# A gated linear recurrence and a gated unit on one core: loads of 1024 tokens, exponentials in pairs, squares per chunk, and new instruction queues

## The chip, the cores and the metric

The kernel runs on one core of a Trainium2 chip. The core has a matrix engine (TensorE, PE in the profile; its weight loads are listed apart as PEld), three engines for elementwise work (VectorE or DVE, ScalarE or ACT, GpSimd or POOL), an engine that issues transfers (SyncE, SP) and 16 DMA engines. Each engine works through its own queue in order, and the queues meet at semaphores. The metric is the device time of one execution in microseconds (us), as the median of several runs. A profile comes from one execution, and its span is the time from the first to the last instruction.

## The reference

Inputs are x, r_gate and i_gate, each 4 sequences of 6336 tokens by 256 channels in float32, a parameter per channel, and the weights of a gated unit. What is computed:

```python
log_a = 8.0 * sigmoid(r_gate) * log(clip(sigmoid(a_param), 1e-6, 1 - 1e-6))
a_t = exp(log_a)
norm = sqrt(max(1 - a_t * a_t, 1e-6))
x_gated = norm * sigmoid(i_gate) * x
h = a_t[:, t] * h + x_gated[:, t]            # for every token t: y[:, t] = h
gate = sigmoid(sum over k of conv_w[k] * y shifted by 4 - k tokens)   # k = 0..4, causal
out = (gate * (y @ w_val)) @ w_out
```

The output is 4 x 6336 x 256 in float32. The inputs come to 78 MB and the output to 26 MB.

## The kernel before

All 25,344 tokens are one line, cut into 51 windows (256, 256, 512, then 512 each, the last 256 long) and 28 chunks. Chunks 0, 1 and 2 are one window, chunks 3 to 25 are two windows of 512, chunks 26 and 27 are one. Window w of chunk c is 2c - 3 or 2c - 2 in the middle. A gate or x is loaded by window with its tokens spread over the 128 partitions: a partition holds J = n/128 neighbouring tokens of 256 channels, 4 KB in one piece for a window of 512. The recurrence runs along tokens with channels on partitions, so a and the gated x are transposed on TensorE.

The whole order is written out in the string ORDER, one word for each step. A word is emitted onto the queue (or queues) of the engines it uses, so the words of an engine, read in the order of ORDER, are that engine's queue. The words, with their functions and lines:

- lr, li, lx (L292, SP): loads of the r gate, the i gate and x into rings of four windows each. st (L546, SP): the store of a window. All four share SP's one queue.
- ta, tb (L310, L313, ScalarE): tanh of the r gate and of the i gate of a chunk, into taring and tbring.
- tr (L357, TensorE): transposes of taring for a group of one or two chunks and one half h of the channels. ex (L378, ScalarE): the exponential of that group, out of PSUM into aring. It scales by khf, which s_kt computes from a_param at the start: a transpose on TensorE, a chain of small steps on VectorE and one exponential on ScalarE.
- sq (L386, GpSimd), sa (L394, ScalarE): squares of a, by chunk and half, into ering. rt (L405, ScalarE): square roots for a batch of up to three chunks. A switch between the table of tanh and exp and that of the square root is a table load (L562).
- pp (L320, GpSimd): adds 1 to the tanh of the i gate. up (L332, GpSimd): multiplies it by x into uring. xp (L337, TensorE) and uv (L346, VectorE) do the same for windows 1, 2 and 6 through PSUM.
- nt (L420, TensorE): transposes of the norms back to tokens. xg (L450, VectorE): multiplies uring by them. xt (L461, TensorE): transposes of the result. sc (L483, VectorE): the recurrence as a scan, by half.
- cv (L495, TensorE), tg (L502, ScalarE): convolution and its tanh. vl (L510, TensorE), gv (L515, VectorE): value matmuls and the gate's product. ou (L525, TensorE): output matmuls. cd (L533, VectorE) and ca (L535, ScalarE): copies of the result out of PSUM.
- wm (L364, TensorE): five matmuls that nobody reads, to keep TensorE warm. s_diag and s_wl, s_wcast prepare the weights of the convolution and of the matmuls.

An element of a transposed norm group is read as one column in nq, where nq is the number of 256-token pieces of a window:

```python
nc.tensor.transpose(out=bank[:, k:k + P], in_=ering[:, e + q:e + wins[w] // 2:nq], identity=ident[:])
```

With windows of 512, nq is 2, and the float32 columns that are read lie 8 bytes apart.

Of the kernel before, what the change touches and what calls it, by code (L numbers as in the profile page):

```python
# [40 lines left out]
ex.2.1 sq.1.0 ta.3 sq.2.1 pp.0 sq.0.0 sq.0.1 ta.4 tb.1 lr.10 tr.3.0@4,5 tb.2 lr.9 lr.8 lr.7 lx.2 tr.3.1@2,3 ex.3.0  # L41
s_wl.1 up.0 lx.1 lx.4 wm.10@6 ex.3.1 sq.3.0 wm.5@6 lx.3 wm.3@6 tb.3 sq.3.1 wm.9@6 wm.6@6 ta.6 pp.4 sq.4.1 ta.5 lr.13
li.5 xp.2@2,3 li.6 sq.4.0 li.7 lr.14 tr.5.0@4,5 lx.6 uv.2 pp.3 rt.0 rt.2 nt.0@0 up.4 xg.0 rt.1 xt.0@0,1 xp.1@2 rt.3
sc.0.0 nt.1@3 up.3 lx.5 nt.2@0 uv.1 s_wl.0 xg.1 xg.2 xt.1@2,3 sc.0.1 lx.7 sc.1.0 nt.3@6,7 lr.12 sc.1.1 xg.3 ex.5.0
xt.2@0,1 sc.2.1 sc.2.0 tb.4 cv.0@2,3 tr.5.1@4,5 xt.3@6,7 lr.11 li.8 sq.5.0 ex.5.1 tg.0 sc.3.0 pp.5 sc.3.1 cv.2@0,1
# [53 lines left out]
cv.48@0,1 st.44 cv.47@6,7 rt.11 xt.27@3 ou.46.0@4,5 xg.26 xg.27 ou.45.0@2,3 tg.47 sc.26.1 sc.26.0 vl.47@6,7 ca.46.0  # L99
gv.47 ca.45.0 tg.48 vl.48@4,5 cv.49@2,3 ou.47.0@0,1 tg.49 vl.49@6,7 sc.27.1 gv.48 sc.27.0 gv.49 st.46 ca.47.0  # L100
ou.48.0@4,5 ca.48.0 st.45 cv.50@0,1 tg.50 st.47 ou.49.0@6,7 ca.49.0 st.48 st.49 vl.50@4,5 gv.50 ou.50.0@4 ca.50.0
st.50
"""


@with_exitstack
def kernel(
# [82 lines left out]
    with tc.manual_schedule():  # L190
# [103 lines left out]
        def op_lr(w):  # L294
            load(w, "r")
# [298 lines left out]
```

## Time and profile before

| what | before |
| --- | --- |
| median of 3 runs | 287.52 us (287.51 to 288.32) |
| span of the profiled execution | 286.4 us (the page gives no other time of it) |
| ScalarE busy | 273.6 us, 96% |
| TensorE busy | 251.8 us, 88% |
| VectorE busy | 246.8 us, 86% |
| GpSimd busy | 241.6 us, 84% |
| bytes moved | 104.76 MB, mean 366 GB/s |

Busy time is a sum over the whole span; what counts in a stretch is read from the rows of that stretch. A row of a stretch gives its start and end, its length, each engine's busy time and instruction count, the granted TensorE clock, the share of time in which the DMA engines were busy and the rate. A row of a timeline gives start, length, engine, line, operation, tiles and shape, a count where neighbours are merged, and in brackets the idle time before it with what ended that. A row of a group gives busy us, the mean ns of one, and idle time. A wait row gives the total in us, how often, and the longest.

### The profile page before, as it was taken

How to read it: one execution, taken by the hardware profiler on the slowest of the kernel's cores; microseconds unless marked ns; L12 is line 12 of the kernel's file. 1: busy time of each engine (PE TensorE's matmuls, PEld its weight loads, DVE VectorE, ACT ScalarE, POOL GpSimd, SP SyncE). 2: the span in 40 equal slices, each digit the busy share in tenths (PEclk: the TensorE clock that was granted, in tenths of full speed). 3: DMA queues.
4: the chain of work that ended last, by engine and by line, in shares of the span. 5: the costliest groups of instructions: out<-in, count | busy, mean ns of one | idle time of the engine just before them, and what ended most of it. 6: DMA issues, size and time to landing. Idle time of an engine off the chain costs nothing.

```text
span 286.4 us, 6382 instructions
## 1 busy us (share of the span) xinstructions
PE 251.8 (88%) x2552; PEld 171.1 (60%) x2576; DVE 246.8 (86%) x214; ACT 273.6 (96%) x198; POOL 241.6 (84%) x161
## 2 busy tenths in 40 slices
PE   1387778899999999988988999989989899999993
PEld 1253447456656767455756676656646774767562
DVE  4002898969999899999999999999999999999991
ACT  5999999999999999999999999999999999898984
POOL 1659589899999999999999999999996999874600
PEclk9999999999999999999999999999999999999999
DMA  7999999999999999999999999999999999994536
GB/s 243 384 373 407 409 403 408 388 366 376 410 408 366 418 367 392 414 410 334 405 364 413 411 332 356 420 416 419 415 401 333 359 416 406 364 356 170 192 150 256
DMA packets 29996, 104.76 MB, mean 366 GB/s; under 512 B 3335, under 2 KB 3854, under 8 KB 29966
## 3 DMA queue, kind: packets, MB, share of 16 engines
q1 hardware_dynamic: 29952, 104.35, 94.5%
q8 instruction: 20, 0.33, 0.5%
q14 instruction: 10, 0.08, 0.1%
q10 hardware_dynamic: 14, 0.01, 0.0%
HBM read 78.39 MB, written 25.95 MB: 364 GB/s over the span
## 4 chain that ended last, share of the span: by engine, by line
ACT 33%; PE 29%; DVE 14%; issue 12%; DMA 8%; SPq 1%; ACTq 0%; DVEq 0%
ACT ering L405 8%; PE banks L495 8%; DVE yring L483 7%; PE banks L525 7%; DMA rring<-in_r_gate_dram 6%; ACT tgring L502 6%; ACT taring L310 5%; ACT tbring L313 5%; ACT aring L378 5%; PE banks L510 5%; PE banks L461 3%; DVE tgring L515 3%; PE banks L420 3%; ACT L562 3%; DVE oring L533 2%
## 5 line engine op out<-in xcount | busy, mean ns | idle before, releaser
L386 POOL TENSOR_TENSOR ering<-aring 128x1024 f32<-128x1024 f32 (+2 forms) x54 | 91.5, 1714 | 16.7 <-ACT aring L378 16.4
L332 POOL TENSOR_TENSOR uring<-tbring,xring 128x1024 bf16<-128x1024 bf16 (+1 forms) x48 | 101.1, 2119 | 3.6 <-DMA xring<-in_x_dram 3.1
L483 DVE TENSOR_TENSOR_SCAN yring<-aring,yring,banks 128x1024 bf16<-128x1024 f32 (+5 forms) x50 | 101.7, 2064 | 2.1 <-PE banks L461 1.9
L495 PE MATMUL banks<-yring,diag 64*64 64x512 bf16 (+7 forms) x1080 | 62.1, 361 | 2.3 <-ACT aring L378 1.6
L515 DVE SCALAR_TENSOR_TENSOR tgring<-tgring,banks 128x1024 bf16<-128x1024 bf16 (+1 forms) x51 | 59.1, 1178 | 4.0 <-PE banks L510 3.4
L320 POOL TENSOR_SCALAR tbring<-tbring 128x1024 bf16<-128x1024 bf16 (+1 forms) x48 | 49.1, 1032 | 6.8 <-ACT tbring L313 6.7
L378 ACT ACTIVATE aring<-banks,khf 128x2048 f32<-128x2048 bf16 (+3 forms) x38 | 54.2, 1476 | 0.4 <-PE banks L357 0.3
L525 PE MATMUL banks<-wo,tgring 128*128 128x256 bf16 x396 | 51.0, 274 | 3.7 <-DVE tgring L515 3.2
L502 ACT ACTIVATE tgring<-banks 128x1024 bf16<-128x1024 f32 (+1 forms) x51 | 50.2, 1011 | 2.0 <-PE banks L495 1.9
L510 PE MATMUL banks<-yring,wv 128*128 128x512 bf16 (+4 forms) x192 | 48.1, 359 | 3.7 <-ACT tgring L502 1.9
L310 ACT ACTIVATE taring<-rring 128x2048 bf16<-128x2048 f32 (+2 forms) x28 | 47.9, 1718 | 1.4 <-DMA rring<-in_r_gate_dram 1.4
L525 PEld LDWEIGHTS <-tgring 128*128 128x128 bf16 x396 | 41.2, 114 | 13.1 <-DVE tgring L515 8.8
L313 ACT ACTIVATE tbring<-iring 128x2048 bf16<-128x2048 f32 (+2 forms) x28 | 48.2, 1726 | 0.0
L405 ACT ACTIVATE ering<-ering 128x4096 bf16<-128x4096 f32 (+5 forms) x16 | 44.8, 2840 | 0.1
L495 PEld LDWEIGHTS <-diag 64*64 64x64 bf16 x1080 | 29.0, 106 | 25.6 <-issue 9.9
L533 DVE COPY oring<-banks 128x1024 f32<-128x1024 f32 (+1 forms) x36 | 41.9, 1182 | 1.4 <-PE banks L525 0.7
L357 PE MATMUL banks<-ident_b,taring 128*128 128x128 bf16 x396 | 29.9, 230 | 9.4 <-ACT taring L310 6.7
L357 PEld LDWEIGHTS <-taring 128*128 128x128 bf16 x396 | 26.5, 103 | 14.2 <-ACT taring L310 7.4
L510 PEld LDWEIGHTS <-wv 128*128 128x128 bf16 x216 | 19.7, 98 | 24.5 <-issue 10.3
L450 DVE TENSOR_TENSOR uring<-banks,uring 128x2048 bf16<-128x2048 bf16 (+2 forms) x26 | 29.4, 1134 | 3.5 <-PE banks L420 3.2
L420 PE MATMUL banks<-ident,ering 128*128 128x128 f32 x192 | 28.3, 289 | 1.1 <-ACT ering L405 0.9
L461 PE MATMUL banks<-ident,uring 128*128 128x128 f32 x192 | 25.9, 276 | 3.5 <-DVE uring L450 2.8
(49 smaller groups left out, 154.0 us busy)
## 6 DMA issues: line engine op xcount, KB each, us to landing
rring<-in_r_gate_dram SPq DMA_DIRECT2D x48, 512.0 KB, 8.2
iring<-in_i_gate_dram SPq DMA_DIRECT2D x48, 512.0 KB, 8.7
xring<-in_x_dram SPq DMA_DIRECT2D x48, 512.0 KB, 8.2
out_dram<-oring SPq DMA_DIRECT2D x48, 512.0 KB, 6.5
rring<-in_r_gate_dram SPq DMA_DIRECT2D x3, 256.0 KB, 4.1
iring<-in_i_gate_dram SPq DMA_DIRECT2D x3, 256.0 KB, 6.5
xring<-in_x_dram SPq DMA_DIRECT2D x3, 256.0 KB, 8.5
out_dram<-oring SPq DMA_DIRECT2D x3, 256.0 KB, 5.2
```

Source lines behind the costliest of these rows:

```text
L310: nc.scalar.activation(**tangent(c, taring, NTR, rring, NRI))
L313: nc.scalar.activation(**tangent(c, tbring, NTI, iring, NII))
L332: nc.gpsimd.tensor_tensor(out=u, in0=t1, in1=xt, op=ALU.mult)
L378: nc.scalar.activation(out=dst, in_=src, func=ACT.Exp, scale=khf[:, h:h + 1], bias=khf[:, h:h + 1])
L386: nc.gpsimd.tensor_tensor(out=e, in0=a, in1=a, op=ALU.mult)
L405: nc.scalar.activation(out=ering[:].bitcast(BF16)[:, 4 * o:4 * o + 2 * n], in_=ering[:, 2 * o:2 * o + 2 * n], func=ACT.Sqrt, scale=-0.25, ...
L483: nc.vector.tensor_tensor_scan(out=yring[:, h, col:col + o1 - o0], data0=aring[:, h, a_at[c] + o0:a_at[c] + o1], data1=xT[:, o0:o1], initi ...
L495: nc.tensor.matmul(out=gp[oh * 64:oh * 64 + 64, h, a:b], lhsT=diag[half * 64:half * 64 + 64, h, k, :], rhs=yring[half * 64:half * 64 + 64, ...
L502: nc.scalar.activation(out=tgring[:, w % NTG, :, 0:wins[w]], in_=live.pop(("gp", w))[:, :, 0:wins[w]], func=ACT.Tanh, scale=0.5)
L510: nc.tensor.matmul(out=val[:, m, a:b], lhsT=wv[:, hk, m * P:(m + 1) * P], rhs=yring[:, hk, col:col + b - a], start=(hk == 0), stop=(hk == ...
L515: nc.vector.scalar_tensor_tensor(out=tgring[:, w % NTG, :, 0:wins[w]], in0=tgring[:, w % NTG, :, 0:wins[w]], scalar=1.0, in1=live.pop(("va ...
L525: nc.tensor.matmul(out=ops[:, j * D:(j + 1) * D], lhsT=gv[:, hk, j:wins[w]:J], rhs=wo[:, hk, :], start=(hk == 0), stop=(hk == H - 1))
```

## The change

- A load takes a whole chunk: 1024 tokens, 1 MB, in one transfer, with 8 neighbouring tokens (8 KB) on a partition. There are 28 loads each of r, i and x instead of 51. Stores stay by window. The x ring takes its slots as the other rings do, at (w + 1) % 4.
- Tokens of a chunk therefore lie in another order: J = 8 where it was 4. tr, ex, nt and xt step accordingly. In nt and xt, nq is that of a chunk, 4 where it was 2.
- Exponentials: chunks 11 and 12, and 21 and 22, were groups of one and are pairs. There are 34 exponentials instead of 38.
- Squares: from chunk 3 to 25 one instruction on GpSimd covers both halves of a chunk. The two squares on ScalarE, sa.25.1 and sa.27.1, go to GpSimd.
- pc adds 1 to the tanh for a whole chunk, and takes the place of 44 of the 48 pp.
- s_kt and s_diag take their PSUM bank from ORDER, and stand in other places.
- All of ORDER is new. Among its differences: 8 wm instead of 17, one copy (ca.35) on ScalarE instead of VectorE, r loads from lr.0 up.

```diff
-GROUPS = [[0], [1], [2], [3, 4], [5, 6], [7, 8], [9, 10], [11], [12], [13, 14], [15, 16], [17, 18], [19, 20], [21],
-    [22], [23, 24], [25], [26], [27]]
+GROUPS = [[0], [1], [2], [3, 4], [5, 6], [7, 8], [9, 10], [11, 12], [13, 14], [15, 16], [17, 18], [19, 20], [21, 22],
+    [23, 24], [25], [26], [27]]
 ORDER = """
-s_ident s_small s_kt s_diag lr.2 lr.0 s_wl.3 lr.1 li.0 lr.3 s_wl.2 ta.2 ta.0 lr.4 tr.0.1@0 tr.2.0@1 lr.6 ta.1 lr.5
-tr.1.0@2 tb.0 tr.0.0@3 li.1 tr.2.1@4 ex.2.0 li.2 tr.1.1@5 li.3 ex.1.1 lx.0 ex.0.1 sq.1.1 li.4 ex.1.0 sq.2.0 ex.0.0
+s_ident lr.0 lr.1 lr.2 s_small li.0 ta.0 lr.3 ta.1 tr.1.1@5 wm.4@7 tr.0.0@1 tr.0.1@0 tr.1.0@7 ta.2 s_kt@2 tb.0 ex.0.0
+tr.2.1@4 ex.2.1 ex.0.1 ex.1.0 lr.4 li.2 lx.0 wm.6@6 wm.1@7 tr.2.0@7 wm.2@4 sq.2.1 ta.3 ex.1.1 pp.0 sq.1.1 up.0 ta.4
+lr.5 lx.1 li.3 tr.3.0@0,1 s_wl.1 s_wl.3 lx.2 li.1 s_wl.0 s_wl.2 lx.3 ex.2.0 tb.2 ex.3.0 sq.2.0 sq.0.1 sq.1.0 sq.0.0
+tr.3.1@4,5 ex.3.1 ta.5 tb.3 tb.1 lr.6 li.4 s_diag@6 xp.2@0,1 xp.1@4 sq.4 sq.3 uv.2 rt.1 rt.0 rt.2 uv.1 nt.1@5 xg.1
...
+        def load(c, which):
+            w, k, n = cwins[c][0], len(cwins[c]), clen[c]
+            ring, slots = {"r": (rring, NRI), "i": (iring, NII), "x": (xring, NX)}[which]
+            at = place(w, slots)
+            dst = ring[:, at:at + k, 0:wins[w] // P, :].rearrange("p w j d -> p (w j) d")
+            nc.sync.dma_start(dst, flat[which][cstart[c]:cstart[c] + n, :].rearrange("(p j) d -> p j d", p=P))
...
+        def op_pc(c):
+            w, k = cwins[c][0], len(cwins[c])
+            t = tbring[:, place(w, NTI):place(w, NTI) + k, 0:wins[w] // P, :].rearrange("p w j d -> p (w j d)")
+            nc.gpsimd.tensor_scalar(out=t, in0=t, scalar1=1.0, scalar2=1.0, op0=ALU.mult, op1=ALU.add)
...
+        def both_squares(c):
+            n = clen[c]
+            return (ering[:, H * e_at[c]:H * (e_at[c] + n)].rearrange("p (h n) -> p h n", h=H),
+                    aring[:, :, a_at[c]:a_at[c] + n])
+
+        def op_sq(c, *h):
+            e, a = squares(c, h[0]) if h else both_squares(c)
             nc.gpsimd.tensor_tensor(out=e, in0=a, in1=a, op=ALU.mult)
...
         def op_nt(c, *at):
             bank = banks[:, at[0]:at[-1] + 1].rearrange("p b n -> p (b n)")
+            k, n = 0, clen[c]
+            nq = n // (2 * P)
+            for q in range(nq):
+                for h in range(H):
+                    e = live["n", c] + h * n // 2
+                    nc.tensor.transpose(out=bank[:, k:k + P], in_=ering[:, e + q:e + n // 2:nq], identity=ident[:])
+                    k += P
...
+            nq = clen[c] // (2 * P)
             for h in range(H):
                 bank = banks[:, at[h]]
+                for u, q in pairs(c):
+                    nc.tensor.transpose(
+                        out=bank[:, q:clen[c] // 2:nq],
+                        in_=u[:, h * P:(h + 1) * P, :].rearrange("p d two -> p (d two)").bitcast(FP32),
+                        identity=ident[:])
```

The stretches of the queues that the prediction speaks of, in the new order:

- TensorE starts with tr.1.1 wm.4 tr.0.0 tr.0.1 tr.1.0 s_kt tr.2.1 wm.6 wm.1 tr.2.0 wm.2 tr.3.0 tr.3.1. Before: s_kt s_diag tr.0.1 tr.2.0 tr.1.0 tr.0.0 tr.2.1 tr.1.1 tr.3.0 tr.3.1.
- ScalarE starts with ta.0 ta.1 ta.2 s_kt tb.0 ex.0.0 ex.2.1 ex.0.1 ex.1.0 ta.3 ex.1.1 ta.4 ex.2.0 tb.2 ex.3.0 ex.3.1 ta.5 tb.3 tb.1 rt.1 rt.0 rt.2 rt.3. Before: s_kt ta.2 ta.0 ta.1 tb.0 ex.2.0 ex.1.1 ex.0.1 ex.1.0 ex.0.0 ex.2.1 ta.3 ta.4 tb.1 tb.2 ex.3.0 ex.3.1 tb.3 ta.6 ta.5 rt.0 rt.2 rt.1 rt.3.
- SP starts with lr.0 lr.1 lr.2 li.0 lr.3 lr.4 li.2 lx.0 lr.5 lx.1 li.3 s_wl.1 s_wl.3 lx.2 li.1 s_wl.0 s_wl.2 lx.3 lr.6 li.4.
- From rt.10 on, TensorE has nt.23 vl.41 vl.40 xt.23 ou.41 ou.39 nt.24 ou.40 cv.42 tr.27.0 vl.42 tr.27.1 nt.25 xt.24 cv.43 ... ou.49 vl.50 ou.50. Before: nt.23 vl.41 vl.40 nt.24 xt.23 ou.39 cv.42 ou.41 ou.40 vl.42 tr.27.1 xt.24 tr.27.0 cv.43 vl.43 nt.25 ... ou.49 vl.50 ou.50.

More of the change, by code (lines that the diff above doesn't have):

```diff
@@ L41 @@
[L41 to L45, printed above, removed]
@@ L103 @@
+ca.50.0 st.50
 """
@@ L229, in s_ident, with s_kt @@
             nc.gpsimd.tensor_copy(out=ident_b[:], in_=ident[:])
-        def s_kt():
-            kps = banks[:, 0]
+        def s_kt(at):
+            kps = banks[:, at]
             nc.tensor.transpose(out=kps[:, 0:H], in_=ap2[0:H, :], identity=ident[0:H, 0:H])
```

213 lines of the change are left out of this document (86 added, 127 removed).

## The prediction

> **What bounds the kernel now.** I read the page first, the span and the busy times.
>
> ```profile
> span 286.4 us, 6382 instructions
> PE 251.8 (88%) x2552; PEld 171.1 (60%) x2576; DVE 246.8 (86%) x214; ACT 273.6 (96%) x198; POOL 241.6 (84%) x161
> ```
>
> The span is 286.4 us; the runs' median is 287.52, so 1.1 us lies around the span, and I add it at the end. ScalarE (ACT) is busiest. Next the stretches, one row each (us; busy time and count per engine, then granted clock, DMA share, GB/s).
>
> ```profile
> 0.00:10.00 10.00, 2.66 (x19) 2.08 (x19) 3.80 (x20) 6.40 (x11) 1.70 (x9) 1.00 0.81 278
> 10.00:20.00 10.00, 5.67 (x39) 4.16 (x40) 0.00 (x0) 9.62 (x9) 6.55 (x8) 1.00 1.02 388
> 20.00:60.00 40.00, 32.63 (x313) 21.31 (x314) 29.68 (x30) 39.63 (x27) 34.64 (x25) 1.00 1.02 402
> 60.00:100.00 40.00, 38.62 (x358) 25.67 (x361) 36.17 (x27) 39.90 (x27) 39.94 (x25) 1.00 1.01 389
> 100.00:244.00 144.00, 134.85 (x1453) 92.36 (x1463) 141.92 (x109) 143.73 (x92) 140.74 (x86) 1.00 1.00 389
> 244.00:280.00 36.00, 35.46 (x365) 24.22 (x369) 34.51 (x29) 31.95 (x35) 18.05 (x13) 1.00 0.67 245
> ```
>
> To be seen: from 20 to 244 ScalarE hardly rests (143.7 of 144 us in the long stretch). Before 60 it idles 3.60 + 0.38 + 0.37 = 4.35 us, nearly all of it in the first 10. VectorE rests 3.8 us in 60 to 100 and 2.1 in the 144 after that; GpSimd is nearly as full (3.1 of 144 idle) and the transfers' share is 1.00. No engine has room, so the middle can become shorter only by less work on ScalarE. From 244 to 280 it is TensorE that is full, 35.46 of 36. The hand-over is in the timelines of ScalarE and TensorE (start, us, what):
>
> ```profile
> 238.87 5.33 ACT L405 ACTIVATE ering<-ering 128x6144 bf16<-128x6144 f32 x1
> ...
> 243.04 1.07 PE L525 MATMUL banks<-wo,tgring 128*128 128x256 bf16 x8
> 244.25 1.23 PE L420 MATMUL banks<-ident,ering 128*128 128x128 f32 x8
> ...
> 248.39 1.04 PE L461 MATMUL banks<-ident,uring 128*128 128x128 f32 x8
> ...
> 282.17 0.61 PE L525 MATMUL banks<-wo,tgring 128*128 128x256 bf16 x4 [0.84 <-DVE tgring L515]
> ```
>
> Square roots rt.10 end at 244.20, and at 244.25 TensorE starts nt.23, the transposes that need them. From there to 282.78 it works nearly without a gap: 38.5 us. Behind nt.23 its queue has the same instructions before and after the change, in another order. So the end is the end of rt.10, plus 38.5 us of TensorE, plus the last copy and store, 3.6 us. And rt.10 ends when ScalarE has done what stands ahead of it. So the sum is ScalarE's work and waits up to rt.10, then TensorE's work behind it.
>
> **ScalarE's work up to rt.10.** I compared the two queues word by word. Same set of tanh, square roots and table loads (14 ahead of rt.10's own, in both), with four differences. Rows (one of the timeline, then groups by shape with busy us and mean ns):
>
> ```profile
> 194.21 4.49 ACT L378 ACTIVATE aring<-banks,khf 128x1024 f32<-128x1024 bf16 x4
> ...
> L378 ACT ACTIVATE aring<-banks,khf 128x2048 f32<-128x2048 bf16 x18 | 36.8, 2074 | 0.0
> L535 ACT COPY oring<-banks 128x1024 f32<-128x1024 f32 x14 | 13.9, 1016 | 2.1 <-PE banks L525 2.0
> L378 ACT ACTIVATE aring<-banks,khf 128x1024 f32<-128x1024 bf16 x10 | 11.4, 1219 | 0.0
> ...
> L394 ACT ACTIVATE ering<-aring 128x1024 f32<-128x1024 f32 x1 | 1.1, 1122 | 0.0
> ```
>
> Four single exponentials in a row took 4.49, not 4 x 1.219 = 4.88, so neighbours overlap by 0.13. The eight single ones (chunks 11, 12, 21, 22) thus cost 8 x 1.09 = 8.7 us, four paired ones 4 x (2.074 - 0.13) = 7.8: **-0.9**. Square sa.25.1 leaves ScalarE, 1.12 - 0.13: **-1.0**. Copy ca.35 comes to it, 1.02 - 0.13: **+0.9**. The other square, sa.27.1, stood behind rt.10 and is worth nothing. The pairs now read PSUM at half the former step. Single ones read at that step already, and (2074 - 1219)/1024 = 0.83 ns per element says that the step is free: 0.
>
> **The start.** Every exponential needs khf, which s_kt makes. Before, s_kt heads TensorE's queue. Now it stands behind tr.1.1, wm.4 and three more tr, so it waits for ta.1, and ta.1 for a load. Rows of before (the ScalarE, VectorE, TensorE and SP timelines):
>
> ```profile
> 0.74 0.52 ACTq L224 DMA_DIRECT2D ap<-in_a_param_dram  x1
> 4.54 1.58 ACT L310 ACTIVATE taring<-rring 128x1024 bf16<-128x1024 f32 x2 [0.49 <-DMA rring<-in_r_gate_dram]
> ...
> 3.46 0.16 DVE L234 COPY ksig<-banks 128x2 f32<-128x2 f32 x1 [3.46 <-PE banks L233]
> 6.64 0.17 DVE L248 TENSOR_SCALAR khf<-ktmp 128x2 f32<-128x2 f32 x1
> ...
> 3.19 0.23 PE L233 MATMUL banks<-ident,ap 2*128 2x2 f32 x1 [3.19 <-DMA ap<-in_a_param_dram]
> 6.94 1.65 PE L357 MATMUL banks<-ident_b,taring 128*128 128x128 bf16 x14 [0.37 <-DVE wcol L256]
> 17.90 6.31 PE L364 MATMUL banks<-ident_b 128*128 128x512 bf16 x25
> ...
> 0.72 0.86 SPq L292 DMA_DIRECT2D rring<-in_r_gate_dram  x2
> ...
> L310 ACT ACTIVATE taring<-rring 128x512 bf16<-128x512 f32 x3 | 1.9, 621 | 0.2 <-DMA rring<-in_r_gate_dram 0.2
> DMA to landing us min/median/max: 3.8/8.0/11.1
> ```
>
> Loads now start with lr.0 and lr.1, issued at 0.72 and 1.15. The 768 KB of before had landed at 4.54; I take 3.8 for the first 256 KB and 4.4 for the second. ta.0 runs to 4.4 and ta.1 to 5.0 (0.62 each). Then TensorE: two transposes 0.24 (1.65/14 each), wm.4 1.26 (five of 6.31/25), six transposes 0.71, s_kt's own 0.23: 7.45. VectorE's chain took 3.46 to 6.81, 3.35 us, so khf is ready at 10.8. ScalarE stands meanwhile: its exponential inside s_kt is queued ahead of tb.0, and all behind that waits for khf. Done by 10.8 are one table load 1.28, ta.0 and ta.1 1.24, ta.2 1.06, that exponential 0.2, tb.0 0.63: 4.4. So it has idled 6.4 us, against 4.35 in the whole start of before: **+2.1**. Bounds: the 1 KB parameter, issued at 0.74, was used at 3.19, so nothing lands within 2.45 us; then lr.1 lands at 3.6, khf comes at 10.0 and the loss is 1.3. If each load takes the 3.8 us that is the least for this ring, khf comes at 11.4 and the loss is 2.6.
>
> Further waits in the start: lr.3 now fills two slots, one of them still held by lr.0, so it waits for ta.0 (before, its first half went out at once). lr.4 waits for ta.2, lr.5 for ta.3, and SP is in order, so li.2 and lx.0 queue behind. I followed it at 400 GB/s (1 MB in 2.6 us), with 2 us from issue to the first byte (1 KB took 2.45): lr.5 is issued at 14.7 and lands at 19.3 for ta.5 at 22.7; li.3 lands at 22 for tb.3 at 24.5; li.1 at 24.7 for tb.1 at 26.3. All in time, with 1.6 us as the least room. Squares of chunks 4 and 3 now wait for both halves (ex.3.1 ends at 22.7) and take 3.6 us each, so rt.3 could start at 29.9; ScalarE arrives at 30.3. Cost 0, up to 1.8 if the cover is gone.
>
> **The middle.** GpSimd, by shape:
>
> ```profile
> L386 POOL TENSOR_TENSOR ering<-aring 128x1024 f32<-128x1024 f32 x45 | 84.4, 1896 | 6.1 <-ACT aring L378 5.8
> L386 POOL TENSOR_TENSOR ering<-aring 128x512 f32<-128x512 f32 x4 | 4.2, 1039 | 2.9 <-ACT aring L378 2.9
> L320 POOL TENSOR_SCALAR tbring<-tbring 128x1024 bf16<-128x1024 bf16 x46 | 47.8, 1050 | 6.8 <-ACT tbring L313 6.7
> L320 POOL TENSOR_SCALAR tbring<-tbring 128x512 bf16<-128x512 bf16 x2 | 1.2, 619 | 0.0
> ```
>
> Squares cost 1.67 ns per element and 0.18 us per instruction, additions 0.84 ns and 0.19. One instruction in place of two saves 0.18 and 0.19 per chunk, 8 us over 22 chunks, less some 2 us for the two squares that come from ScalarE. ScalarE has no wait there that this could end: 0. VectorE loses one copy and does uv.2 and uv.1 earlier, beside idle time: 0, since ScalarE sets rt.10. Nine of 17 warming groups go, 11 us of TensorE; it has gaps there, and the clock stood at 1.00 in the stretch after the last of them: 0. Loads are half as many issues of twice the size. ScalarE waited 1.4 us in all for the r ring, and the start's waits are counted above: 0, with a price in the rivals.
>
> **The norm's transposes.** nt now reads ering at a step of 16 bytes, not 8 (one column in nq, and nq goes from 2 to 4). Groups of eight: nt.23 took 1.23 us, xt.23, which reads adjacent elements, 1.04.
>
> ```profile
> L420 PEld LDWEIGHTS banks<-ident,ering x192: 140/209/223, 28.5 to 258.1; 128*128 128x128 f32 x192
> L420 PE MATMUL banks<-ident,ering x192: 272/283/389, 28.6 to 258.2; 128*128 128x128 f32 x192
> ...
> L461 PEld LDWEIGHTS banks<-ident,uring x192: 137/141/152, 29.6 to 262.3; 128*128 128x128 f32 x192
> L461 PE MATMUL banks<-ident,uring x192: 270/273/329, 29.6 to 262.4; 128*128 128x128 f32 x192
> ```
>
> Less the last one (0.283 and 0.273), that is a pace of 0.135 and 0.110 us. Weight loads take 209 ns at 8 bytes and 141 adjacent. Doubling the step cost 0.025; from 8 to 16 bytes, by bytes spanned, twice that, 0.05. In the middle TensorE's gaps and the lost warming groups cover it. Behind rt.10 nothing does: 24 transposes (nt.23 to nt.25), **+1.2**. Bounds: 0 if the step no longer matters, 24 x 0.138 = 3.3 if the pace takes the whole growth of the weight load (two more times 69 ns). A gain is excluded, since 8 bytes are dearer than 4. [...] xt writes PSUM at double the step too; its matmuls that write adjacent words (chunks 0 and 1, nq = 1) are among the shortest, 270, and the median is 273: 0.
>
> **Sum.** -0.9 - 1.0 + 0.9 + 2.1 + 1.2 = +2.3 on the span: 288.7, and with 1.1 around it 289.8 us.
>
> **Rivals.**
>
> A, the forecast: khf late, transposes dearer, 289.8. Its own range goes from 288.4, where B ends, to 289.8 + 0.5 + 2.1 = 292.4, with both upper bounds. Chance 0.52.
>
> B, no change: the loss at the start is at its lower end (1.3) and the wider step is free: 287.52 - 1.0 + 1.3 = 287.8. For it speaks that the loss rests on landing times not seen alone. Chance 0.18. I call it no change within 0.3% (0.86 us), about what a measurement of this kernel can tell.
>
> C, loads become the bound. A slot pair must be empty before 1 MB can be asked for, x had single slots until now. By my walk 11.0 MB have landed at 33.3 us, where the rows of before give 2.78 + 3.88 + 5.35 = 12.0; and with a share of 1.00 to 1.02 at 389 to 402 GB/s the 2.5 us are hard to make good. Against it: SP itself waits on compute (its waits by releaser, then its and ScalarE's timelines, then the page's issues).
>
> ```profile
> SPq L292 <- ACT taring L310: 24.5, 11, 4.6
> ...
> 195.21 2.72 SPq L292 DMA_DIRECT2D rring<-in_r_gate_dram  x3
> ...
> 213.09 1.90 ACT L310 ACTIVATE taring<-rring 128x2048 bf16<-128x2048 f32 x1
> ...
> rring<-in_r_gate_dram SPq DMA_DIRECT2D x48, 512.0 KB, 8.2
> ```
>
> The three issues at 195.21 hold lr.44 and lr.43: out by 197.9 and landed some 8.2 later, 206, they had 7 us before ta.23 read them at 213.1. C decides when a load comes more than 7 us later than now. Then 0.1 us on each of some 40 r and i loads makes +4: 293.8. Chance 0.18.
>
> D, faster: GpSimd paced the middle, at 39.94 of 40 in 60 to 100, and ScalarE's full rows only follow it. Then it runs as fast as VectorE lets it, which rested 2.1 us in 100 to 244, and the start's loss is absorbed: 287.5 - 2.1 = 285.4. It decides if ScalarE has idle time in the middle of the new profile while the end comes earlier. Against it: ScalarE waits for nothing there, and its durations are work. Chance 0.12. [...]
>
> **Numbers.** Time 289.8. Faster is D, 0.12; same is B, 0.18; slower is A and C, 0.70. The range leaves out D and the far end of C: 287.0 to 294.0.
>
> **What would show it.** ScalarE idle near 6 us in the first 11, its first exponential near 10.8; rt.10 ending near 245.3; no idle over 0.5 us per 40 between 20 and 240; nt's weight loads well over 209 ns and a group of eight near 1.6 us; TensorE 39.7 us behind rt.10; GpSimd some 6 us less busy. Wrong if khf comes before 9.6, if ScalarE waits for rring or iring in the middle, or if nt keeps its 1.23.

## The result, and the profile after

The changed kernel takes 300.44 us in the median, against 287.92 for the kernel before on the same chip: 1.043 times as long, 95% interval 1.038 to 1.048. Of its four executions one, at 306.74 us, fell in a slower state (with it the median is 301.15); medians and ratios, here and below, are of the other, fast ones. I forecast 289.8 (287.0 to 294.0). The sign was right, the size was not: +12.5 us where I had +2.3. The profiled execution took 300.44 us, with a span of 298.7. First the page's busy times, then two rows of stretches: the whole time up to rt.10's first instruction, after and before (start:end, length, then busy time and count of PE, PEld, DVE, ACT and POOL, granted clock, DMA share, GB/s).

```profile
span 298.7 us, 6120 instructions
...
PE 249.0 (83%) x2531; PEld 169.8 (57%) x2531; DVE 247.4 (83%) x213; ACT 272.7 (91%) x193; POOL 237.7 (80%) x118
```

```profile
0.00:250.36 250.36, 206.51 (x2097) 141.43 (x2101) 207.49 (x180) 233.43 (x156) 213.18 (x103) 0.96 0.95 369
```

```profile
0.00:238.87 238.87, 209.36 (x2123) 142.69 (x2146) 206.44 (x181) 234.15 (x161) 218.42 (x146) 1.00 1.00 386
```

To be seen: up to rt.10, which starts 11.5 us later, ScalarE worked 0.7 us less than before (233.43 against 234.15) and stood still for 16.9 us instead of 4.7. Nearly all of the loss is waiting ahead of rt.10. What comes behind is about as long as before. The timeline of TensorE after:

```profile
255.75 1.23 PE L409 MATMUL banks<-ident,ering 128*128 128x128 f32 x8 [0.47 <-ACT ering L396]
...
293.91 0.61 PE L512 MATMUL banks<-wo,tgring 128*128 128x256 bf16 x4 [0.84 <-DVE tgring L502]
```

From nt.23's start to the last output matmul's end it is 38.8 us (38.5 before; I had forecast 39.7), and a group of eight norm transposes still takes 1.23. Where ScalarE waits is shown by its wait view (operation and what released it: us in total, times, longest) and its timeline, both of the changed kernel:

```profile
ACT taring L298 <- DMA rring<-in_r_gate_dram: 5.2, 3, 2.2
ACT aring L372 <- POOL ering L385: 4.6, 3, 1.9
ACT tgring L489 <- PE banks L482: 4.0, 5, 1.6
...
ACT aring L372 <- DVE khf L239: 2.3, 1, 2.3
```

```profile
6.94 1.06 ACT L298 ACTIVATE taring<-rring 128x1024 bf16<-128x1024 f32 x1 [2.23 <-DMA rring<-in_r_gate_dram]
...
11.47 2.14 ACT L372 ACTIVATE aring<-banks,khf 128x256 f32<-128x256 bf16 x4 [2.35 <-DVE khf L239]
...
39.05 0.60 ACT L489 ACTIVATE tgring<-banks 128x512 bf16<-128x512 f32 x1 [1.62 <-PE banks L482]
...
54.11 4.00 ACT L372 ACTIVATE aring<-banks,khf 128x2048 f32<-128x2048 bf16 x2 [1.06 <-POOL ering L385]
...
83.82 1.91 ACT L298 ACTIVATE taring<-rring 128x2048 bf16<-128x2048 f32 x1 [1.55 <-DMA rring<-in_r_gate_dram]
...
117.74 4.01 ACT L372 ACTIVATE aring<-banks,khf 128x2048 f32<-128x2048 bf16 x2 [1.85 <-POOL ering L385]
...
124.63 1.02 ACT L489 ACTIVATE tgring<-banks 128x1024 bf16<-128x1024 f32 x1 [1.08 <-PE banks L482]
...
243.31 1.20 ACT L372 ACTIVATE aring<-banks,khf 128x1024 f32<-128x1024 bf16 x1 [1.66 <-POOL ering L385]
...
250.36 5.33 ACT L396 ACTIVATE ering<-ering 128x6144 bf16<-128x6144 f32 x1
```

Three sorts of wait are new. In the first 12 us: ta.2 for its load and the first exponential for khf. ScalarE is busy 4.84 us there, 8.40 before (the rows of after and before):

```profile
0.00:12.00 12.00, 4.69 (x23) 2.37 (x24) 2.77 (x17) 4.84 (x8) 0.97 (x7) 1.00 0.78 268
0.00:12.00 12.00, 2.66 (x19) 2.08 (x19) 3.80 (x20) 8.40 (x13) 3.69 (x11) 1.00 0.84 295
```

Then exponentials that wait for GpSimd: 1.06, 1.85 and 1.66 us. And a handful of waits for the r ring (83.82) and for the convolution's matmuls (39.05, 124.63). These three sorts come to 3.6 + 4.6 + 4.2 = 12.4 us, about the 12.2 by which ScalarE stood still longer ahead of rt.10. The stretches of the middle say the same; where I had said "no idle over 0.5 us per 40", ScalarE lacks 1.9 to 3.0 us in three of four:

```profile
20.00:60.00 40.00, 28.76 (x254) 19.11 (x254) 27.59 (x30) 37.26 (x26) 30.64 (x18) 0.87 0.95 382
60.00:100.00 40.00, 33.49 (x318) 22.28 (x318) 34.62 (x26) 38.11 (x24) 38.14 (x17) 0.96 0.97 365
100.00:140.00 40.00, 34.30 (x367) 24.05 (x369) 35.10 (x30) 37.00 (x23) 35.74 (x15) 0.96 0.91 349
140.00:180.00 40.00, 37.19 (x422) 26.05 (x412) 39.62 (x31) 39.94 (x26) 36.09 (x15) 1.00 1.02 423
```

### The profile page after: what moved, and what is told of

Read it like the earlier page. It is cut to its first block, busy times and chain, and to the rows that moved or that the text cites. A ratio compares the mean times of both kernels' runs of the same rounds, so it can differ in the third digit from the quotient of the medians.

```text
span 298.7 us, 6120 instructions
## 1 busy us (share of the span) xinstructions
PE 249.0 (83%) x2531; PEld 169.8 (57%) x2531; DVE 247.4 (83%) x213; ACT 272.7 (91%) x193; POOL 237.7 (80%) x118
## 5 line engine op out<-in xcount | busy, mean ns | idle before, releaser
L385 POOL TENSOR_TENSOR ering<-aring 128x2048 f32<-128x2048 f32 (+2 forms) x33 | 90.2, 2747 | 24.2 <-ACT aring L372 23.1
L372 ACT ACTIVATE aring<-banks,khf 128x2048 f32<-128x2048 bf16 (+3 forms) x34 | 53.1, 1599 | 7.5 <-POOL ering L385 4.6
L497 PE MATMUL banks<-yring,wv 128*128 128x512 bf16 (+4 forms) x216 | 50.3, 364 | 7.5 <-ACT tgring L489 4.0
L512 PEld LDWEIGHTS <-tgring 128*128 128x128 bf16 x396 | 42.3, 115 | 17.7 <-DVE tgring L502 8.2
L314 POOL TENSOR_SCALAR tbring<-tbring 128x2048 bf16<-128x2048 bf16 x22 | 41.8, 1900 | 4.9 <-ACT tbring L301 4.9
L520 DVE COPY oring<-banks 128x1024 f32<-128x1024 f32 (+1 forms) x35 | 40.7, 1184 | 3.7 <-PE banks L512 3.7
L351 PE MATMUL banks<-ident_b,taring 128*128 128x128 bf16 x396 | 29.2, 229 | 7.6 <-ACT taring L298 6.5
L351 PEld LDWEIGHTS <-taring 128*128 128x128 bf16 x396 | 25.8, 103 | 13.9 <-ACT taring L298 7.1
L409 PEld LDWEIGHTS banks<-ident,ering 128*128 128x128 f32 x192 | 26.2, 209 | 6.4 <-ACT ering L396 2.5
```

The source lines that it names most:

```text
L351: nc.tensor.transpose(out=bank[:, o:o + P], in_=taring[:, place(w, NTR), j, h * P:(h + 1) * P], identity=ident_b[:])
L372: nc.scalar.activation(out=dst, in_=src, func=ACT.Exp, scale=khf[:, h:h + 1], bias=khf[:, h:h + 1])
L385: nc.gpsimd.tensor_tensor(out=e, in0=a, in1=a, op=ALU.mult)
L497: nc.tensor.matmul(out=val[:, m, a:b], lhsT=wv[:, hk, m * P:(m + 1) * P], rhs=yring[:, hk, col:col + b - a], start=(hk == 0), stop=(hk == ...
L512: nc.tensor.matmul(out=ops[:, j * D:(j + 1) * D], lhsT=gv[:, hk, j:wins[w]:J], rhs=wo[:, hk, :], start=(hk == 0), stop=(hk == H - 1))
```

## The experiments

Eighteen kernels ran. Those whose names begin with x start from the changed kernel, those with b from the kernel before, which took 287.6 to 287.8 us in the runs beside them. Ratios are to that kernel, with 95% intervals.

### Squares by half, s_kt early, warm TensorE: one at a time and together

x1_split:

```diff
-sq.4 sq.3 ... sq.25
+sq.4.1 sq.4.0 sq.3.1 sq.3.0 ... sq.25.1 sq.25.0
```

> The changed kernel with every square of a whole chunk written as two words, one per half, at the same place (22 instructions more on GpSimd, about 0.18 us each). Theory F (false neighbour): a square over both halves of a chunk reads two stretches of aring that lie 5120 columns apart; the exponentials that come next in the program write a place that lies between them, not in them, and wait for that square all the same. Then the three waits of exponentials for GpSimd (1.06, 1.85 and 1.66 us) are gone, ScalarE's rows for 20 to 60, 100 to 140 and 220 to 260 rise by 1 to 2 us each, and the time falls by 2.5 to 4.6 us, to 296.5 to 298.7. Rival L (GpSimd is simply late with squares that the exponential must wait for, because it overwrites what they read): the waits stay, GpSimd has 4 us more to do, time 301 to 303.

x2_kt:

```diff
-s_small li.0 ta.0 lr.3 ta.1 tr.1.1@5 wm.4@7 tr.0.0@1 tr.0.1@0 tr.1.0@7 ta.2 s_kt@2 tb.0
+s_small s_kt@2 li.0 ta.0 lr.3 ta.1 tr.1.1@5 wm.4@7 tr.0.0@1 tr.0.1@0 tr.1.0@7 ta.2 tb.0
```

> The changed kernel with s_kt moved ahead to right behind s_small, so that it heads TensorE's queue as before; nothing else. Theory K: khf is ready near 6.9 instead of 11.37, the first exponential comes near 8.5, ScalarE idles 4.5 to 5 us in the first 12 instead of 7.2, and the time falls by 2 to 2.8 us, to 298.4 to 299.2. Rival: what ScalarE gains it loses again at the next loads (ta.3 or ta.4 then wait for the r ring) or at the first convolution (the wait for TensorE at 39.05 grows from 1.62 to over 3), and the time stays at 300.5 to 301.5.

x3_warm:

```diff
-s_diag@6 xp.2@0,1
+s_diag@6 wm.10@7 wm.11@7 wm.12@7 wm.13@7 xp.2@0,1
```

> The changed kernel with four groups of five dummy matmuls more, between s_diag and the first xp, in the 5.7 us in which TensorE had nothing to do (19.9 to 25.6). Theory W: the granted clock in 24 to 40 is 1.00 instead of 0.57 to 0.86, six xp matmuls take 2.9 us instead of 5.46, the wait of the first tg for the first cv (1.62 us at 39.05) is gone, time 1.2 to 2 us less: 299 to 300. Rival: the clock rises, but the wait is set by the late squares and square roots (rt.3 starts at 30.6 either way), and the time stays within 0.5 us of 301.2.

x4_all has the three edits at once.

> The three edits together: squares by half, s_kt early, four groups of dummy matmuls. If the three are separate losses ahead of rt.10, their gains add up: 4.6 + 2.5 + 1.6 = 8.7 us at most, 292.5 to 295. If they hide one another (a queue that comes earlier meets the next wait, for the r ring at 83.82 or for cv at 124.63), the time is 295 to 299.

Measured: x1_split 296.68 us (1.0317, 1.0297 to 1.0337), x2_kt 298.25 (1.0381, 1.035 to 1.0413), x3_warm 300.2 (1.0407, 1.0371 to 1.0443), x4_all 292.86 (1.0183, 1.0145 to 1.0222). Against the 300.44 of the changed kernel (1.0431, 1.0378 to 1.0484) that is -3.8, -2.2, -0.2 and -7.6. Only x1_split and x4_all lie clear of its interval; x2_kt and x3_warm overlap it. The single gains come to 6.2 against 7.6 together: within these intervals they add up, and no more than that is shown. In the profiled executions rt.10 starts at 244.77, 247.32, 251.75 and 241.56, in the changed kernel at 250.36: -5.6, -3.0, +1.4 and -8.8.

The wait view of ScalarE in x1_split, its largest rows:

```profile
ACT taring L300 <- DMA rring<-in_r_gate_dram: 4.6, 3, 1.8
ACT oring L524 <- PE banks L514: 3.8, 5, 1.5
ACT aring L374 <- DVE khf L241: 2.3, 1, 2.3
ACT tgring L491 <- PE banks L484: 2.3, 4, 1.0
ACT ering L398 <- POOL ering L387: 1.9, 1, 1.9
```

No exponential waits for GpSimd any more, though GpSimd has 22 instructions more to do, and the gain, 3.8 us, is near the sum of the three waits, 4.6. That speaks for theory F, and against L, by which shorter squares would have gained nothing. In x2_kt and x3_warm, whose squares are long, three such waits stay (5.4 and 4.6 us); in x4_all there is none. Still, GpSimd is late once in x1_split: the square roots rt.6 now wait 1.9 us for it.

x2_kt shows the start. VectorE in the changed kernel, then in x2_kt:

```profile
11.20 0.17 DVE L239 TENSOR_SCALAR khf<-ktmp 128x2 f32<-128x2 f32 x1
```

```profile
5.61 0.17 DVE L239 TENSOR_SCALAR khf<-ktmp 128x2 f32<-128x2 f32 x1
```

khf comes 5.6 us earlier. The first exponential comes only 3.1 us earlier, at 8.38, since ta.2 (6.90) and tb.0 stand ahead of it:

```profile
6.90 1.06 ACT L298 ACTIVATE taring<-rring 128x1024 bf16<-128x1024 f32 x1 [2.26 <-DMA rring<-in_r_gate_dram]
...
8.38 2.12 ACT L372 ACTIVATE aring<-banks,khf 128x256 f32<-128x256 bf16 x4
```

rt.10 starts 3.0 us earlier in this profile, so there the later waits don't eat the gain. The time is 2.2 us less, with intervals that overlap.

x3_warm moved the clock and hardly the time. The stretch from 20 to 60 in x3_warm:

```profile
20.00:60.00 40.00, 31.73 (x302) 20.45 (x300) 27.18 (x30) 38.22 (x27) 31.63 (x19) 1.00 0.97 389
```

The granted clock is 1.00 where it was 0.87, and the time is 0.2 us less, far inside the spread. The wait at 39.05 is gone, but in its profile a load comes later: ScalarE's longest wait for the r ring is 3.3 us, at 85. So by itself warmth gains nothing that can be told from the spread.

### Is it the span of an instruction, or its length?

aring has two halves of 5120 columns one behind the other. A square over both halves of chunk 6, which lies at 4096, touches 4096 to 5119 and 9216 to 10239, and what it spans is everything from 4096 to 10239. ex.7.1 at 54.11 writes columns 5120 to 7167, between the two; it starts when GpSimd ends the squares of chunks 6 and 5 (46.92 and 7.16 us long). Nothing it overwrites is read by them. The profile reads such a wait from a semaphore, so it stands in the program; by what rule it got there, no run shows. To tell this from mere length, x5_layout keeps the long squares and moves the halves together:

```diff
-aring = rings.tile([P, H, NA], FP32, name="aring")        # half h of chunk c starts at [:, h, a_at[c]]
+aring = rings.tile([P, H * NA], FP32, name="aring")       # half h of chunk c at H * a_at[c] + h * clen[c]
```

> The changed kernel with its long squares kept, but aring laid out chunk by chunk (half 0 and half 1 of a chunk side by side), so that the stretch a square spans holds nothing of other chunks. Theory F: the three waits of exponentials for GpSimd are gone as with two short squares, and GpSimd has 4 us less to do than there: 295.5 to 297.2. Rival: it was the length of the instruction (3.6 against 1.9 us) that made ScalarE wait, then the waits stay and the time is 300 to 302.

Its time is 299.18 us (1.0371, 1.0302 to 1.0439), not to be told from the changed kernel's: neither what F gave nor, in its waits, what the rival gave.

```profile
ACT taring L298 <- DMA rring<-in_r_gate_dram: 4.3, 3, 2.1
...
ACT aring L370 <- DVE yring L468: 3.9, 2, 2.6
```

The waits for GpSimd, 4.6 us in the changed kernel, are gone with each square still over both halves (one takes 3.60 us in the changed kernel, and 3.60 in b5_both_layout below, which has this layout too), so length wasn't what made these exponentials wait. In their place two exponentials wait 3.9 us for VectorE's scans: in this layout the pairs 11, 12 and 21, 22, which wrap round the ring, span nearly all of it, both halves of every other chunk included. The longer of the two, ex.21.1, starts at 203.85, when a scan of chunk 18 ends; the pair overwrites nothing of chunk 18. The same cause, one place on; I had not seen it coming.

b1_both puts the long squares alone into the kernel before, and b5_both_layout adds the other layout to that:

```diff
-sq.6.1 ... sq.6.0        # every chunk from 3 to 24
+... sq.6                 # both halves, at the place of the later word
```

> The kernel before with one part of the change alone: the squares of chunks 3 to 24 over both halves in one GpSimd instruction, at the place of the later of the two words. Theory F: four exponentials then wait for GpSimd (ex.7.1, ex.13.1, ex.19.1 and one of chunk 25), which none did before; ScalarE has no slack there, so the time rises by 1 to 4 us, to 288.6 to 291.6. Rival: GpSimd saves 0.18 us per chunk, the exponentials find it done, time 287.6 within 0.5.

> The kernel before with the squares of chunks 3 to 24 over both halves as in b1_both (306.2), same order of words, but aring laid out chunk by chunk, so that the stretch of such a square holds nothing of another chunk. Theory F: of b1_both's 18.5 us all that came from false neighbours goes, in both directions (exponentials that wait for squares, and squares that wait for the exponentials of another pair, as the one at 76.00 that waited 5.5 us); what stays is the real wait of a square for its second half; 287 to 290. Rival: the later place of the squares is what cost the time (GpSimd gets its work too late), then it stays at 303 to 306.

b1_both takes 306.18 us (1.0629, 1.0588 to 1.0669), far more than the 1 to 4 I gave it, and b5_both_layout 295.34 (1.0271, 1.024 to 1.0302), more than my 287 to 290. The waits that I had expected, of exponentials for GpSimd, come to only 1.9 us in b1_both. The timelines of GpSimd and ScalarE in b1_both show why the first is so dear:

```profile
76.00 3.60 POOL L387 TENSOR_TENSOR ering<-aring 128x2048 f32<-128x2048 f32 x1 [5.53 <-ACT aring L374]
```

```profile
73.85 4.01 ACT L374 ACTIVATE aring<-banks,khf 128x2048 f32<-128x2048 bf16 x2
77.73 1.04 ACT L503 ACTIVATE tgring<-banks 128x1024 bf16<-128x1024 f32 x1
84.84 1.91 ACT L309 ACTIVATE tbring<-iring 128x2048 bf16<-128x2048 f32 x1 [6.07 <-POOL uring L328]
```

It holds in the other direction too. The square of chunk 8 stands behind ex.9.0 in the program, and what it spans holds that exponential's place; so GpSimd idles 5.53 us until ex.9.0 has run, though chunk 8 has been complete since 53.15. Then tb waits 6.07 us for a multiply that is late on GpSimd. With the halves side by side that is gone. ScalarE from 60 to 100, first b1_both, then b5_both_layout:

```profile
60.00:100.00 40.00, 34.58 (x307) 22.82 (x304) 31.09 (x23) 33.88 (x21) 32.36 (x17) 0.91 0.88 317
```

```profile
60.00:100.00 40.00, 38.70 (x364) 25.72 (x366) 36.34 (x28) 39.91 (x27) 38.08 (x21) 1.00 1.01 391
```

Of the 18.5 us of b1_both, 10.9 go with the layout. The other 7.6 stay: there the later place of the squares, which then wait for their real second half, is the candidate, and no run shows it.

### The clock and the warming groups, by themselves

b3_nowarm takes the groups wm.10, wm.5, wm.3, wm.9 and wm.6 out of the kernel before.

> The kernel before without the 25 dummy matmuls at 17.9 to 24.2 us, nothing else. My prediction counted lost warming groups as 0. Theory W: the granted clock in 24 to 40 falls to 0.6 to 0.9, the xp matmuls and the first transposes take twice as long, the first cv is late; ScalarE has about 1.5 us of other work in front of the first tg, so the time is 0 to 2 us longer, 287.6 to 289.6, and I take 288.3.

It takes 288.06 us (1.0014, 0.9992 to 1.0036): no difference that can be told. From 20 to 40 its clock is 0.83 (1.00 before), and ScalarE is as busy as ever (19.94 us, 19.66 before):

```profile
20.00:40.00 20.00, 13.03 (x123) 8.78 (x127) 11.13 (x15) 19.94 (x15) 15.84 (x14) 0.83 1.03 405
```

### What is left: transfers?

x7_halves is x4_all with each 1 MB load as two of 512 KB:

```diff
-nc.sync.dma_start(dst, src)
+for v in range(k):
+    nc.sync.dma_start(ring[:, at + v, 0:J, :], src[:, v * J:(v + 1) * J, :])
```

> The version with the three edits (292.9), with each load of a 1024-token chunk issued as two transfers of 512 KB in 4 KB pieces, back to back, into the same slots: order, slots and waits as they are. Theory: the large transfers cost nothing by themselves, ScalarE's waits for the r ring stay at 2 to 4 us in sum, time 292 to 294. Rival (loads as the bound, by their size): transfers of half the size land earlier by 1 us or more, the waits for the r ring shrink under 1 us, time 290 to 291.5.

x8_best has the other layout, the wrapped pairs as two instructions, s_kt early, the warming groups and the halved loads:

> The changed kernel with s_kt early, four warming groups more, loads in halves, and aring laid out chunk by chunk, the two pairs that wrap round the ring written as two instructions per half; long squares kept. Theory F: ScalarE waits neither for GpSimd nor for VectorE's scans before its exponentials, GpSimd has 4 us less to do than with short squares; time as x7_halves (291.2) or up to 1 us less: 290 to 291.5. If more than false neighbours is behind the waits, 293 or more.

x9_loads changes the order of loads in it, and x10_1mb goes back from there to transfers of 1 MB:

```diff
-lr.5 lx.1 li.3 tr.3.0@0,1 s_wl.1 s_wl.3 lx.2 li.1 s_wl.0 s_wl.2 lx.3 ... ta.10 ta.9
+lr.5 li.3 li.1 tr.3.0@0,1 lx.1 lx.2 lx.3 s_wl.1 s_wl.3 s_wl.0 s_wl.2 ... ta.9 ta.10
```

> As x8_best, with two changes in the order of loads: li.3 and li.1 ahead of lx.1 and the weights, and ta.9 ahead of ta.10, so that lr.11 (which needs ta.9's slots) can be issued 1.9 us earlier. Theory: in x8_best ScalarE lost 2.5 us in 20 to 60 and 1.9 in 60 to 100 against the kernel before, at tb.3, tb.1, the first tg and ta.11, all behind loads that come late in SP's order; with these gone rt.10 starts near 239.5 and the time is 288 to 290. Rival: other loads are late in their place (lx.1 and lx.2 for the xp matmuls, so the first tg), time 291 or more.

> As x9_loads, with each 1024-token load as one transfer of 1 MB again. If the size of the transfer costs nothing by itself, within 1 us of x9_loads; if a 1 MB transfer that must land whole before its first use costs ScalarE time, 1.5 to 3 us more than x9_loads, with waits for the r or i ring.

Measured: x7_halves 291.19 us (1.0113, 1.0067 to 1.0159), x8_best 294.54 (1.0254, 1.0214 to 1.0294), x9_loads 293.19 (1.0189, 1.0168 to 1.0211), x10_1mb 292.46 (1.0164, 1.014 to 1.0188). Halving the transfers took 1.7 us off x4_all, and undoing it took 0.7 off x9_loads: no effect of the size that holds in both. Nor did ScalarE's waits for the r ring shrink as the rival for x7_halves had it: 5.6 us in its profile, 2.7 in that of x4_all. In x8_best no exponential waits for GpSimd or VectorE, yet it is 3.4 us slower than x7_halves with its short squares. Its two wrapped pairs are four more exponentials, 0.5 us for each pair by the rows of the pair 21, 22 in x7_halves and in x8_best:

```profile
197.65 4.01 ACT L376 ACTIVATE aring<-banks,khf 128x2048 f32<-128x2048 bf16 x2 [0.28 <-issue]
```

```profile
198.44 4.49 ACT L372 ACTIVATE aring<-banks,khf 128x1024 f32<-128x1024 bf16 x4 [0.23 <-PE banks L353]
```

That is 1.0 of the 3.4 us. By my own expectation, 293 or more means that more than false neighbours is behind the waits; what it is stays open. The new order of loads gave 1.3 us of the 5 or so I had hoped for: the waits moved to ta.6, the first tg and still ta.11.

Then the amount. By 60 us the kernel before had moved 22.7 MB (360 GB/s to 33.3 us, 402 from there), the changed one 20.6 (323 and 370), x10_1mb 21.7 (343 and 384). b10_more adds four stores to the kernel before, x13_less takes two loads out of x10_1mb:

```diff
-st.7
+st.7 xtra.7      # window 7 once more, to a spare tensor; so 9, 10 and 11
```

> The kernel before with four stores more: the output windows 7, 9, 10 and 11 are each written a second time, to a spare tensor (4 x 512 KB at 85 to 125 us; nothing else changes). 2.1 MB more are 5.4 us of the transfers' time at 390 GB/s. Theory C (the transfers, at a share of 1.00 from 20 to 240, have no room, and what they lose at one place is paid at the end): 290.3 to 293, ScalarE waits for the r or i ring behind 100. Rival: loads run far enough ahead of ScalarE to hide it, 287.5 to 288.5.

> As x10_1mb (292.5), with the loads lx.5 and lx.6 left out, so that two chunks multiply the x of earlier ones: 2.1 MB less to move between 35 and 65 us. Theory C: what stays lost in x10_1mb is that its transfers were 1.05 MB behind those of the kernel before at 60 us (21.7 against 22.7 MB); then the wait of ta.11 (0.99 us) and the later ones for r and i go, time 289.5 to 291. Rival: the order of the words holds ScalarE, not the rate, time 292 to 293.

b10_more takes 288.2 us (1.002, 1.0007 to 1.0033), x13_less 292.48 (1.015, 1.0123 to 1.0178), the same as the 292.46 of x10_1mb. Neither 2.1 MB more nor 2.1 MB less is worth anything like their 5.4 us. From 100 to 140 b10_more moves more than before (414 against 385 GB/s), and ScalarE stays full (the rows of before and b10_more):

```profile
100.00:140.00 40.00, 37.33 (x406) 25.69 (x408) 39.11 (x31) 39.94 (x25) 39.77 (x25) 1.00 1.01 385
100.00:140.00 40.00, 37.20 (x406) 25.47 (x406) 39.11 (x31) 39.94 (x26) 39.75 (x25) 1.00 1.02 414
```

So the rate isn't the bound in the kernel before, though the share reads 1.01, and by x13_less not in x10_1mb either. What holds ta.11 can be read in x13_less, in SP's timeline and ScalarE's:

```profile
70.89 2.13 SPq L280 DMA_DIRECT2D rring<-in_r_gate_dram  x2
```

```profile
68.95 3.71 ACT L298 ACTIVATE taring<-rring 128x2048 bf16<-128x2048 f32 x2
...
79.70 1.91 ACT L298 ACTIVATE taring<-rring 128x2048 bf16<-128x2048 f32 x1 [1.34 <-DMA rring<-in_r_gate_dram]
```

Its load can go out only when ta.9 (the first of the two at 68.95, over near 70.8) has emptied the slots; it goes out at 70.89, and ta.11 starts 8.8 us later. ScalarE has 7.5 us of other work in between. In the kernel before, the same two tanh started at 66.08 and ta.11 at 78.97, with three more instructions between. By these rows it is the order of ScalarE's own words; moving ta.11 was not tried.

### The gains that I had booked on ScalarE

b4_sq25 and b8_sq25 give sa.25.1 to GpSimd in the kernel before; b7_pair and b9_pair pair chunks 21 and 22 on top.

```diff
-sa.25.1 ... sq.25.0 pp.44 pp.43 pp.45 up.44 pp.46 ... up.43
+sq.25.0 sq.25.1 pp.44 pp.43 up.44 ... up.43 pp.45 pp.46        # b8_sq25
```

```diff
-tr.21.0@0 tr.21.1@1 ... ex.21.0 tr.22.1@6 xt.18@4,5 tr.22.0@0 sc.18.1 sc.18.0 ... ex.21.1 ... ex.22.1 ex.22.0
+tr.21.0@0,1 ... ex.21.0 tr.21.1@6,7 ex.21.1 xt.18@4,5 sc.18.1 sc.18.0 ...                      # b9_pair, on top
```

> The kernel before with the square sa.25.1 given from ScalarE to GpSimd, behind sq.25.0, and up.43 moved ahead of pp.45: the term of -1.0 in my sum, by itself. GpSimd then ends its squares at about 237.6, and rt.10's first instruction would start at 237.9 instead of 238.87: 0.5 to 1.0 us less, 286.7 to 287.2. Rival: GpSimd is late with the sixth square or with up.43, time 287.7 to 289.

> As b4_sq25, and the exponentials of chunks 21 and 22 as one pair (two of 2048 columns for four of 1024), placed ahead of the scans of chunk 18, which their stretch covers. Half of the -0.9 of my sum: 0.5 us less than b4_sq25, 286.2 to 286.8. Rival: the pair waits for the later of its two transposes or for a scan, and gains nothing: 286.7 to 288.

> The kernel before with sa.25.1 given to GpSimd behind sq.25.0, and pp.45 and pp.46 moved behind up.43 so that up.43 isn't late; every load where it was. (In b4_sq25 and b7_pair up.43 stood ahead of its own load lx.43, so it multiplied the x that was in the slot, and lx.43 waited for it: they don't measure this term.) The term of -1.0 by itself: rt.10's first instruction at 237.9 instead of 238.87, time 286.7 to 287.2. Rival: GpSimd is late, 287.7 or more.

> As b8_sq25, with the exponentials of chunks 21 and 22 as one pair ahead of the scans of chunk 18: 0.5 us less than b8_sq25, 286.2 to 286.8. Rival: the pair waits for its later transpose or for the squares or scans that its stretch covers, and the time is b8_sq25's or 1 to 3 us more (b7_pair stood 3 us above b4_sq25).

b4_sq25 (296.96 us) and b7_pair (299.95) multiply a stale x in one window and hold up its load, as the text of b8_sq25 says. b8_sq25 takes 288.77 us (1.0032, 1.0016 to 1.0047), b9_pair 291.05 (1.0113, 1.01 to 1.0127). ScalarE in b8_sq25:

```profile
236.66 1.02 ACT L501 ACTIVATE tgring<-banks 128x1024 bf16<-128x1024 f32 x1 [0.97 <-PE banks L524]
...
238.99 5.33 ACT L404 ACTIVATE ering<-ering 128x6144 bf16<-128x6144 f32 x1
```

The square's 1.1 us are off ScalarE, and 0.97 of them come back at once as a wait for TensorE. rt.10 starts at 238.99, before at 238.87. The 1.0 us by which b8_sq25 is longer lies behind rt.10 (TensorE 39.6 us there, 38.5 before), and it is GpSimd's: with one square more a multiply is late, and VectorE waits for it.

```profile
250.21 1.23 DVE L449 TENSOR_TENSOR uring<-banks,uring 128x2048 bf16<-128x2048 bf16 x1 [1.01 <-POOL uring L331]
```

In b9_pair the pair waits 1.16 us for its transposes, and tg's follow. No version beat the kernel before.

## Why the prediction was wrong, step by step

**The bound.** "So the end is the end of rt.10, plus 38.5 us of TensorE, plus the last copy and store" held: 38.8 us, and 11.5 of the span's 12.3 us lie ahead of rt.10. As a recipe it was right; the waits in front were missing. Of its constants, 1.1 us around the span was too small: 300.44 against 298.7 is 1.7.

**ScalarE's work**, -0.9 - 1.0 + 0.9 = -1.0: measured -0.7 (233.43 against 234.15). As busy time it was about right. That less work is an earlier end was not: in the kernel before, b8_sq25 and b9_pair turn it into waits.

**The start**, +2.1 with 2.6 at most: khf came at 11.37 (I had 10.8, at most 11.4). ScalarE idles 7.2 us of the first 12, 3.6 before: +3.6. The mechanism was right (in x2_kt the first exponential comes 3.1 us earlier), the term too small by 1.5: besides the later khf, I had set the idle time of the first 11 us against that of the first 60 of before, 4.35.

**The middle** is the step that failed: "ScalarE has no wait there that this could end: 0." I priced the long square by its own duration (3.60 us measured, against 2 x 1.896; that was right) and did not ask who waits for it. Such a square, which covers two stretches, holds up exponentials that write what lies between them: three waits, 4.6 us in all, and splitting the squares gives back 3.8 us (x1_split). That is the largest single part of the 10.2 us by which the forecast fell short. ("3.1 of 144 idle" for GpSimd in the prediction should read 3.3, without effect.)

**Loads**, 0 with rival C at +4: ScalarE did wait for the r ring where I named it as a sign of error. C's cause, the rate, fell with b10_more and x13_less. Of its price, the waits themselves in the profile come to 1.55 us behind the start (5.2 in all).

**The warming groups**, 0: right in time (b3_nowarm, x3_warm), wrong in its reason, that "the clock stood at 1.00": without them it was 0.83 from 20 to 40.

**The norm's transposes**, +1.2: measured 0. TensorE's weight loads and matmuls at a step of 16 bytes, in the changed kernel:

```profile
L409 PEld LDWEIGHTS banks<-ident,ering x192: 194/209/232, 30.0 to 266.7; 128*128 128x128 f32 x192
L409 PE MATMUL banks<-ident,ering x192: 271/283/422, 30.8 to 266.8; 128*128 128x128 f32 x192
```

209 and 283 ns in the median are what the step of 8 bytes took. That the pace would grow with the bytes spanned, by 0.05 us for each transpose, was my estimate from the two steps of before; from 8 to 16 bytes it didn't grow.

**B** and **D** fell: the loss at the start was above its upper end, and GpSimd, though 4 us less busy, now holds up ScalarE at three places, so nothing became faster.

**What stays open.** s_kt, squares and warming give back 7.6 of 12.5 us. The other 5 lie, by the waits of the profiles, in loads and first convolutions. Neither the order of loads (1.3 us), nor the size of a transfer, nor the amount moved accounts for them; the order of the words on ScalarE does at ta.11, by its rows, and whether it does for the rest is not known. Part of it differs from execution to execution: x10_1mb and x13_less have the same words in the first 20 us, and ScalarE is busy 15.50 us of them in one profile and 13.48 in the other.

## What to carry to other kernels

Before two instructions become one with a strided operand, look at what lies between its stretches and who touches that: each of them may become a wait, in both directions (here 4.6 us of exponentials that waited for squares, and in b1_both one square that waited 5.53 us for an exponential). Splitting the instruction took the waits of the exponentials away here (x1_split); moving its parts side by side took these away too, but cost others, 3.9 us (x5_layout). Price a merged or moved instruction by who waits for it, not by its own duration alone. A busy engine that loses a microsecond of work gains it only if the next instruction's input is there, and if the engine that takes the work over has room: in b8_sq25 ScalarE lost 1.1 us of work, waited 0.97 of it, and rt.10 came 0.1 us later.

## What was not expected of the hardware

The granted clock of TensorE did not stay at 1.00. In the changed kernel TensorE had nothing to do from 19.9 to 25.6 us; the clock then read 0.50 from 25 to 31, and the xp matmuls took 0.91 us each (six in 5.46) instead of 0.49 (four in 1.95 in the kernel before). It fell again from 34.9 to 38.2, when TensorE had rested for 1.4 us.

```profile
25.00:31.00 6.00, 5.41 (x7) 2.24 (x8) 1.46 (x2) 5.97 (x7) 6.00 (x3) 0.50 1.05 405
34.90:38.20 3.30, 2.70 (x12) 2.42 (x12) 2.69 (x5) 2.52 (x2) 1.71 (x1) 0.50 1.02 417
```

Between the two falls the clock was back at 1.00 from 31.5, 5.9 us after the first of the xp. How long TensorE had rested doesn't tell by itself that the clock falls: in the kernel before it rested 1.69 us ahead of 25.90, longer than ahead of the second fall here, and the clock read 1.00 from 24 to 40. What sets it, no run shows. And a DMA share of 1.01 left room: from 100 to 140 b10_more put 414 GB/s through where 385 had read 1.01.
